# Top-k attention with a PReLU MLP: fewer semaphore waits of VectorE on itself, ScalarE's exits moved, filler matmuls, output parts paced

## The chip, the cores and the metric

One core of a Trainium2 chip. The metric is device time in microseconds, lower is better: the median of three timed executions. A profiled execution of the same kernel gives the trace. Engines: PE is TensorE (matmuls), PEld its weight load, DVE VectorE, ACT ScalarE, POOL GpSimd, SP the engine that issues most DMAs. A core's engines run side by side, each through its own program in order, and wait for one another at semaphores.

## The reference

```
scores = (q @ k^T) / sqrt(64)                  # batch 8, heads 8, seq 576, head_dim 64
kth    = 32nd largest score of each row
attn   = softmax of the scores >= kth, others dropped
x      = attn @ v, heads side by side          # 4608 tokens x 512
h      = x @ w_in                              # 512 x 2048
g      = max(h, 0) + alpha * min(h, 0)
out    = g @ w_out                             # 2048 x 512
```

## The kernel before

The score rows are cut into 144 "duos": two tiles of 128 rows by 576 columns. For each batch there are 16 duos of two heads with the same 128 rows, and 2 that collect the last 64 rows of four heads (their scores take 12 matmuls instead of 6, their products with v 20 instead of 10). The main loop runs over slots n, and one slot holds a step of several duos at once, so that the engines overlap:

- PE, in this order: `st_av(n-5)` (xo, weights times v), `h_pe` (ph: 8 matmuls of x @ w_in for a part of the MLP), the last 64 columns of the scores of duo n+1 (in `st_exit_1`), `o_pe` (pz: 5 matmuls, a quarter of an output tile), transposes of the next q and k (tps), `st_qk(n+2)` (ps_sc: the other score columns), `lin` (plin: in slots 16 to 23 half of one of four 128-row pieces of w_in * alpha @ w_out), and a second `o_pe` if over 10 parts are queued.
- ACT: the two Signs of duo n-1 (sg; they count the scores above a threshold), `st_exit_1(n+1)` (copies the second score tile out of PSUM to s_sb), two Relus of duo n-2 (r), `st_exit_0(n+1)` (the first score tile), the Exp of duo n-3 (w), copies of tps, and `o_act`, the copy of a finished output tile (o_sb<-pz).
- POOL: y = s * sg of duo n-1, and the two subtractions that follow the Relus.
- DVE, `dve_slot(n)`: the top 32 of each row. Twelve MAX8 over 96 columns each go by turns to `up` (SBUF) and to `lo` in `small`; two min/max steps merge them (bot and th); MAX8 of bot fills th; `eq` prepares the choice for duo n-1; `neg` is -th; MAX8 of neg gives the threshold p; two MAX8 over 576 columns of y refine duo n-1. In between lie the softmax normalisation (rz, x) and gT<-ph, the Relu of the MLP.

`small` is one PSUM tile of 160 columns that holds lo, th, n8, eq and io9. Each instruction that writes it waits for the one before that touched it. The scores have one PSUM buffer (`ps_s`, three banks), ph and tps share two (`ps_h`, tag "h"), and plin and pz share one (`ps_z`). Parts of the output queue in `oq`, each with the number of gT pieces that it needs. All engine calls go through a helper, so every instruction has line 31, and it keeps each engine in the order in which the code is written.

Of the kernel before, what the change touches and what calls it, by code (L numbers as in the profile page):

```python
# [16 lines left out]
BIG = float(2.0 ** 60)  # L17
NG = 6
# [17 lines left out]
def fast_path(tc, q, k, v, moe_w_in, moe_w_out, moe_alpha, out, flag):  # L36
    nc = tc.nc
    B, H, S, D = q.shape
# [22 lines left out]
    on = lambda m: 0 <= m < ND  # L61

    with ExitStack() as ctx:
# [6 lines left out]
        two = pool("two", 2)  # L70
# [6 lines left out]
        ps_h = pool("ps_h", 2, space=PSUM)  # L77
# [27 lines left out]

        small = ps_d.tile([128, 160], FP32, name="small")
        io9 = small[:, 146:155]
        for i in range(9):
            DVE.memset(io9[:, i:i + 1], float(2 * i - 63 + S))
        KT = const.tile([128, 2 * ND], FP32, name="KT")  # L110
        v1s = [const.tile([128, 5, 2, 65], BF16, name=f"v1_{i}") for i in range(2 * KPB)]
        ws = [const.tile([128, 2, 640], BF16, name=f"w_{i}") for i in range(3)]
# [4 lines left out]
        w_lin_b = [const.tile([128, DMODEL], BF16, name=f"w_lin_b{i}") for i in range(4)]  # L117
# [39 lines left out]
        T = {}  # L157
# [29 lines left out]
        def st_exit_0(n):  # L187
            ACT.copy(T["s", n][:, 0, :], T.pop(("ps", n))[:, 0:S])
# [6 lines left out]
        def dve_slot(n, f_late):  # L195

            lo = small[:, 0:48].rearrange("p (i g c) -> p i g c", i=2, g=NG // 2)
            th = small[:, 48:112].rearrange("p (i c) -> p i c", i=2)  # L200
            n8 = small[:, 112:128].rearrange("p (i c) -> p i c", i=2)
            eq = small[:, 128:146].rearrange("p (i c) -> p i c", i=2)
            if on(n):
                s = T["s", n]
                up = two.tile([128, 2, NG // 2, 8], FP32, name="up", tag="up")
                for i in range(2):
                    for g in range(NG):
                        DVE.max(out=(lo if g % 2 else up)[:, i, g // 2, :],
                                in_=s[:, i, GW * g:GW * g + GW])
                        if i == 0 and g == 1:  # L210
                            kt_sum(n - 2)
                if on(n - 5):
                    norm_a(n - 5)


                bot = two.tile([128, 2, NG // 2, 8], FP32, name="bot", tag="bot")
                DVE.tensor_tensor(bot, up, lo[:, :, :, ::-1], ALU.min)
                DVE.tensor_tensor(th[:, :, 0:24].rearrange("p i (g c) -> p i g c", g=NG // 2), up,
                                  lo[:, :, :, ::-1], ALU.max)
                if on(n - 5):  # L220
                    norm_b(n - 5)
                for i in range(2):
                    DVE.max(out=th[:, i, 24:32], in_=bot[:, i, :, :])
            else:
                kt_sum(n - 2)
                if on(n - 5):
                    norm_a(n - 5)
                    norm_b(n - 5)
            if on(n - 1):
                y, p9, cs = T.pop(("y", n - 1)), T.pop(("p9", n - 1)), T.pop(("cs", n - 1))  # L230
                DVE.tensor_tensor(eq, io9.unsqueeze(1).to_broadcast([128, 2, 9]),
                                  cs.unsqueeze(2).to_broadcast([128, 2, 9]), ALU.is_equal)
            if on(n):
                neg = two.tile([128, 2, 32], FP32, name="neg", tag="neg")
                DVE.tensor_scalar(neg, th, -1.0, None, ALU.mult)
            if on(n - 1):
                DVE.max(out=p9[:, 0, 1:9], in_=y[:, 0, :])
            h_dve()
            if on(n):
                for i in range(2):  # L240
                    DVE.max(out=n8[:, i, :], in_=neg[:, i, 0:31])
            if on(n - 1):
                DVE.max(out=p9[:, 1, 1:9], in_=y[:, 1, :])
            if on(n):
                p9n = three.tile([128, 2, 9], FP32, name="p9", tag="p9", bufs=4)
                DVE.tensor_scalar(p9n[:, :, 0:1], n8[:, :, 7:8], -1.0, None, ALU.mult)
                T["p9", n] = p9n
            if f_late:
                h_pe()
                h_dve()  # L250
            if on(n - 1):
                pk = two.tile([128, 2, 9], FP32, name="pk", tag="pk")
                DVE.scalar_tensor_tensor(out=pk, in0=eq, scalar=BIG, in1=p9, op0=ALU.mult, op1=ALU.mult)
                T["pk", n - 1] = pk

        def st_count(n):
# [12 lines left out]
                POOL.tensor_tensor(y[:, i, :], T["s", n][:, i, :], sg[:, i, :], ALU.mult)  # L269
            T["y", n] = y  # L270

        def st_relu(n):
            s = T["s", n]
            r = two.tile([128, 2, S], BF16, name="r", tag="sg", bufs=3)
            for i in range(2):
                ACT.activation(r[:, i, :], s[:, i, :], AF.Relu, bias=KT[:, 2 * n + i:2 * n + i + 1], scale=-BIG)
            T["r", n] = r

        def st_sub(n):
            s, r = T["s", n], T.pop(("r", n))  # L280
            for i in range(2):
                POOL.tensor_tensor(s[:, i, :], s[:, i, :], r[:, i, :], ALU.subtract)

        def st_exp(n):
            w = ws[n % 3]
# [82 lines left out]
        soon, hq, oq, act, stores, now = [], [], [], [], [], [0]  # L368
# [38 lines left out]
        def h_pe():  # L407
            while soon and soon[0][0] <= now[0]:
                hq.append(soon.pop(0)[1])
            if hq and wi_free and not act:  # L410
                hq.pop(0)()

        def h_dve():
            if act:
# [2 lines left out]
                ch["done"] += e_n  # L417

        def o_pe():
            if lin_done and oq and oq[0][0]["done"] >= oq[0][1]:  # L420
                oq.pop(0)[2]()

        def o_act():

# [42 lines left out]
        hold, lin_done, wi_free = {}, [], []  # L467
# [17 lines left out]
        def lin(kk, a):  # L485
            if a == 0:
                hold["z"] = ps_z.tile([128, DMODEL], FP32, name="plin", tag="z")
            z = hold["z"]
            for f in range(8 * a, 8 * a + 8):
                PE.matmul(z, hold["wi", kk // 2][:, f, 128 * (kk % 2):128 * (kk % 2) + 128],  # L490
                          hold["wl", f // 8][:, f % 8, :], start=(f == 0), stop=(f == NFT - 1))
            if a == 1:
                ACT.copy(w_lin_b[kk], z)
                if kk == 1:
                    wi_free.append(1)
                if kk == 3:
                    lin_done.append(1)


        for i in range(4):  # L500
# [4 lines left out]
        for kk in range(4):  # L505
            at((13, 14, 17, 18)[kk], "ld", lambda kk=kk: in_trans(kk))
            for a in range(2):
                at(16 + 2 * kk + a, "lin", lambda kk=kk, a=a: lin(kk, a))

        def run(n, kind, most=99):  # L510
            l = todo.get((n, kind), [])
            for f in l[:most]:
                f()
            if l[most:]:
                todo.setdefault((n + 1, kind), [])[0:0] = l[most:]
# [32 lines left out]
        for n in range(ND + 6):  # L548
            end = n >= ND
            now[0] = n  # L550
            run(n, "ld")
            o_sp()

            if on(n - 5):
                st_av(n - 5)
            h_pe()
            late = len(hq) > (12 if n < 104 else 5) or end

            if on(n - 1):
                st_count(n - 1)  # L560
                st_y(n - 1)
            if on(n + 1):
                st_exit_1(n + 1)
            o_pe()
            run(n, "w")

            dve_slot(n, late)
            if on(n - 2):
                st_relu(n - 2)
                st_sub(n - 2)  # L570
            run(n, "cast")
            if on(n + 1):
                st_exit_0(n + 1)
            if n < 2:
                prep_all(2 + n, ACT.copy, ACT.copy, ACT.copy)
            run(n, "prep", 1)
            if on(n + 2):
                st_qk(n + 2)
            run(n, "lin")
            if len(oq) > 10 or end:  # L580
                o_pe()
            if on(n - 3):
                st_exp(n - 3)
# [304 lines left out]
```

## Time and profile before

| | |
|---|---|
| median of 3 runs (lowest, highest) | 975.07 us (974.66 to 975.44) |
| the profiled execution's own time | 979.5 us |
| its span in the trace | 977.7 us |
| busy: DVE, ACT, PE, POOL | 841.0, 798.5, 790.2, 748.7 us |
| mean granted clock of TensorE | 0.932 of full speed |

Busy time of an engine is the union of its instructions' times. DVE instructions overlap at their ends, so the distance from start to start is what one costs, not its duration.

### The profile page before, as it was taken

What the parts mean: (1) busy time and instruction counts of PE and PEld (TensorE: products, weight loads), DVE (VectorE), ACT (ScalarE), POOL (GpSimd) and SP (SyncE); (2) the same over time, 40 slices, a digit from 0 to 9 for tenths busy, and PEclk for the clock granted to TensorE, in tenths of its full rate; (3) what the DMA queues carried; (4) which work ended last, traced back from release to release, by engine and by line L of the source; (5) the groups of instructions that cost most, each with busy time, mean ns of one, the idle gap of its engine ahead of it and who ended that gap; (6) DMA issues with size and microseconds to landing.
All of it is one profiled execution on the core that took longest, in us unless ns stands there. A gap on an engine that the chain in (4) does not pass through costs nothing.

```text
span 977.7 us, 18322 instructions
## 1 busy us (share of the span) xinstructions
PE 790.2 (81%) x5141; PEld 474.4 (49%) x5214; DVE 841.0 (86%) x4063; ACT 798.5 (82%) x1448; POOL 748.7 (77%) x662
## 2 busy tenths in 40 slices
PE   7657768887898878887889787978889688988786
PEld 5334434454464535554455454645455454555453
DVE  3869986689898989899999998999999999899951
ACT  3779985789798978899889897989798998788840
POOL 1788875588787878698888797889788898787840
PEclk9999688899897999798999997999999999799999
DMA  7687763345564454454555464544455443334351
GB/s 160 166 170 155 136 127 72 76 87 107 85 117 91 93 109 96 87 128 85 120 96 116 83 119 91 102 97 106 100 117 106 91 84 71 66 73 65 79 94 42
DMA packets 341006, 99.35 MB, mean 102 GB/s; under 512 B 333712, under 2 KB 333728, under 8 KB 340896
## 3 DMA queue, kind: packets, MB, share of 16 engines
q1 hardware_dynamic: 337888, 95.40, 48.1%
q0 software_dynamic: 608, 2.11, 1.3%
q10 hardware_dynamic: 2400, 0.59, 0.3%
q8 instruction: 43, 0.70, 0.3%
q14 instruction: 67, 0.55, 0.2%
HBM read 36.71 MB, written 9.44 MB: 47 GB/s over the span
## 4 chain that ended last, share of the span: by engine, by line
DVE 57%; PE 20%; ACT 12%; issue 4%; DMA 3%; POOL 1%; another core or an unknown queue 1%; SPq 1%; DVEq 0%; ACTq 0%; POOLq 0%
DVE small L31 18%; DVE p L31 15%; DVE up L31 8%; PE ps_sc L31 7%; PE pz L31 6%; DVE gT L31 6%; ACT sg L31 4%; ACT s_sb L31 3%; ACT r L31 3%; PE xo L31 3%; DVE neg L31 2%; DMA wT<-w 2%; DVE x L31 2%; PE ph L31 2%; PE plin L31 2%
## 5 line engine op out<-in xcount | busy, mean ns | idle before, releaser
L31 POOL TENSOR_TENSOR y<-s_sb,sg 128x576 f32<-128x576 f32 x288 | 362.0, 1278 | 190.6 <-ACT sg L31 188.7
L31 PE MATMUL ps_sc<-qkT 64*128 64x128 f32 (+7 forms) x1280 | 296.7, 511 | 145.6 <-ACT s_sb L31 142.2
L31 POOL TENSOR_TENSOR s_sb<-s_sb,r 128x576 f32<-128x576 f32 x288 | 362.5, 1280 | 2.3 <-ACT r L31 2.2
L31 PEld LDWEIGHTS ps_sc<-qkT 64*128 64x128 f32 (+1 forms) x1280 | 161.1, 200 | 298.7 <-ACT s_sb L31 200.7
L31 ACT ACTIVATE sg<-s_sb,p 128x576 bf16<-128x576 f32 x288 | 221.0, 770 | 50.8 <-DVE p L31 50.6
L31 DVE MAX8 p<-y 128x8 f32<-128x576 f32 x288 | 215.4, 748 | 2.7 <-POOL y L31 2.3
L31 DVE MAX8 small<-s_sb 128x8 f32<-128x96 f32 x864 | 216.1, 250 | 0.0
L31 DVE MAX8 up<-s_sb 128x8 f32<-128x96 f32 x864 | 211.7, 245 | 1.9 <-ACT s_sb L31 1.9
L31 ACT ACTIVATE r<-s_sb,KT 128x576 bf16<-128x576 f32 x288 | 207.9, 772 | 2.9 <-DVE KT L31 2.9
L31 ACT COPY s_sb<-ps_sc 128x576 f32<-128x576 f32 x288 | 180.0, 625 | 33.2 <-PE ps_sc L31 32.9
L31 ACT ACTIVATE w<-s_sb 128x1152 bf16<-128x1152 f32 x144 | 168.3, 1169 | 1.0 <-POOL s_sb L31 1.0
L31 PE MATMUL pz<-w_out_b,gT 128*128 128x512 bf16 x567 | 156.6, 400 | 12.8 <-issue 10.5
L31 PE MATMUL ph<-xT,w_in_b 128*128 128x256 bf16 (+1 forms) x1216 | 155.8, 274 | 0.1
L31 PE MATMUL xo<-v,wT 128*128 128x65 bf16 (+3 forms) x1600 | 132.1, 203 | 12.5 <-DMA wT<-w 12.5
L31 PEld LDWEIGHTS <-wT 128*128 128x128 bf16 (+3 forms) x1600 | 95.6, 102 | 67.6 <-DMA wT<-w 14.1
L31 PEld LDWEIGHTS <-w_in_b 128*128 128x128 bf16 x1216 | 105.7, 99 | 20.1
L31 DVE TENSOR_SCALAR gT<-ph 128x512 bf16<-128x512 f32 x144 | 97.2, 675 | 17.0 <-PE ph L31 16.9
L31 PEld LDWEIGHTS <-gT 128*128 128x128 bf16 x576 | 58.6, 102 | 65.2 <-issue 14.2
L31 DVE RECIPROCAL rz<-xo 128x2 f32<-128x2 f32 x144 | 22.7, 158 | 52.6 <-PE xo L31 52.6
L31 ACT COPY o_sb<-pz 128x512 f32<-128x512 f32 x36 | 21.1, 586 | 55.5 <-PE pz L31 47.5
L31 DVE MAX8 small<-neg 128x8 f32<-128x31 f32 x288 | 56.5, 196 | 5.0
L31 DVE MAX8 small<-bot 128x8 f32<-128x24 f32 x288 | 54.5, 189 | 5.2
(47 smaller groups left out, 578.5 us busy)
## 6 DMA issues: line engine op xcount, KB each, us to landing
k_st<-in_k_dram SPq DMA_DIRECT2D x64, 128.0 KB, 2.8
v_st<-in_v_dram SPq DMA_DIRECT2D x64, 128.0 KB, 2.6
out_dram<-o_sb SPq DMA_DIRECT2D x32, 256.0 KB, 2.3
q_st<-in_q_dram SPq DMA_DIRECT2D x60, 128.0 KB, 2.7
w_st<-in_moe_w_out_dram SPq DMA_DIRECT2D x4, 1024.0 KB, 6.4
wT<-w SPq DMA_TRANSPOSE x144, 3.5
w_in_b<-in_moe_w_in_dram POOLq DMA_DIRECT2D x4, 512.0 KB, 6.5
k_st<-in_k_dram SPq DMA_DIRECT2D x32, 32.0 KB, 2.6
```

The costliest lines, as they stand in the source:

```text
L31: return self.tc.keep_in_program_order(f(*a, **kw))
```

## The change

Six edits, all in the attention path:

1. The dependencies on `small` are declared by columns (`sm`): an instruction keeps only the waits for those that share columns (or bot, neg, p9) with it.
2. `st_relu` and `st_sub` become one function per tile, and `st_exit_0` is written between the two Relus.
3. `keep_warm`: four bf16 matmuls of 512 columns into a PSUM tile of tag "h" that nobody reads, after `h_pe` where that had nothing to do, and after `st_qk` where `o_pe` had nothing to do and there is no `lin`.
4. The second `o_pe` of a slot runs only if over 9 parts are ready, and not for the last quarter of a tile.
5. The copy w_lin_b<-plin moves one slot later, behind the second Relu.
6. `o_pe` and `h_pe` return whether they did something.

```diff
+        def sm(ins, reads, writes):
+            meet = lambda x, y: x == y if str in (type(x), type(y)) else x[0] < y[1] and y[0] < x[1]
+            hit = lambda a, b: any(meet(x, y) for x in a for y in b)
+            keep = [r[0] for r in recent
+                    if hit(writes, r[1]) or hit(writes, r[2]) or hit(reads, r[2])]
+            tc.declare_no_dep(ins.ins, group="small", keep=keep, reason="other columns")
+            tc.add_to_no_dep_group("small", ins.ins)
+            recent.append((ins.ins, reads, writes))
...
-                    DVE.max(out=th[:, i, 24:32], in_=bot[:, i, :, :])
+                    o = 48 + 32 * i
+                    sm(DVE.max(out=th[:, i, 24:32], in_=bot[:, i, :, :]), [f"bot{n % 2}"], [(o + 24, o + 32)])
...
+        def ready():
+            k = 0
+            while lin_done and k < len(oq) and oq[k][0]["done"] >= oq[k][1]:
+                k += 1
+            return k
+
+        def keep_warm():
+            ps = ps_h.tile([128, 512], FP32, name="idle", tag="h")
+            for i in range(4):
+                PE.matmul(ps, v1s[0][:, 0, :, :].rearrange("p a b -> p (a b)")[:, 0:128], ws[0][:, 0, 0:512],
+                          start=(i == 0), stop=(i == 3))
...
+        def lin_out(kk):
+            ACT.copy(w_lin_b[kk], hold["z"])
...
+            at(18 + 2 * kk, "lin_out", lambda kk=kk: lin_out(kk))
...
-            h_pe()
+            if not h_pe() and not end and n > 3:
+                keep_warm()
...
-            o_pe()
+            did = o_pe()
...
             if on(n - 2):
-                st_relu(n - 2)
-                st_sub(n - 2)
-            run(n, "cast")
+                st_relu(n - 2, 0)
             if on(n + 1):
                 st_exit_0(n + 1)
+            if on(n - 2):
+                st_relu(n - 2, 1)
+            run(n, "cast")
+            run(n, "lin_out")
...
-            run(n, "lin")
-            if len(oq) > 10 or end:
+            if (n, "lin") in todo:
+                run(n, "lin")
+            elif not did and not end and n > 3:
+                keep_warm()
+            elif end or (ready() > 9 and oq[0][1] < NFT):
                 o_pe()
```

On VectorE, in a slot of the middle of the program, these stood from the normalisation x to the threshold's MAX8 (in brackets the semaphores waited for; DVE_49 is VectorE's own):

```order
L31 TENSOR_TENSOR x<-xo,rz 128x128 [waits DVE_49]
L31 MAX small<-bot 128x8 [waits DVE_49] x2
L31 TENSOR_TENSOR small<-small,cs 128x18 [waits DVE_49,Activation_49]
L31 TENSOR_SCALAR neg<-small 128x64 [waits DVE_49]
L31 MAX p_7194<-y 128x8 [waits Pool_49]
L31 TENSOR_SCALAR gT<-ph 128x512 [waits PE_49]
L31 MAX small<-neg 128x8 [waits DVE_49] x2
```

and now stand:

```order
L31 TENSOR_TENSOR x<-xo,rz 128x128 [waits DVE_49]
L31 MAX small<-bot 128x8 [waits DVE_49]
L31 MAX small<-bot 128x8
L31 TENSOR_TENSOR small<-small,cs 128x18 [waits Activation_49]
L31 TENSOR_SCALAR neg<-small 128x64 [waits DVE_49]
L31 MAX p_6755<-y 128x8 [waits Pool_49]
L31 TENSOR_SCALAR gT<-ph 128x512 [waits PE_49]
L31 MAX small<-neg 128x8 [waits DVE_49]
L31 MAX small<-neg 128x8
```

The order is the same; the second MAX8 of bot, `eq` (small<-small,cs) and the second MAX8 of neg lost their wait on VectorE, and so did the MAX8 from s_sb into `small`, six in a slot, above these. `neg` still waits, now for the MAX8 of bot.

On ScalarE these stood in slot 17, where the first piece of w_lin was copied:

```order
L31 COPY s_sb<-ps_sc 128x576 [waits PE_49,Activation_49]
L31 ACTIVATE r<-s_sb,KT 128x576 [waits DVE_49,Pool_49]
L31 ACTIVATE r<-s_sb,KT 128x576
L31 COPY s_sb<-ps_sc 128x576 [waits PE_49]
L31 CAST w_lin_b_154<-plin 128x512 [waits PE_49]
```

and now in slot 18:

```order
L31 COPY s_sb<-ps_sc 128x576 [waits PE_49,Activation_49]
L31 ACTIVATE r<-s_sb,KT 128x576 [waits DVE_49,Pool_49]
L31 COPY s_sb<-ps_sc 128x576 [waits PE_49]
L31 ACTIVATE r<-s_sb,KT 128x576
L31 CAST w_lin_b_154<-plin 128x512
```

The second exit stands ahead of the second Relu in every slot, and the cast comes a slot after its matmuls, behind the Relus.

On PE behind the scores of duo 36 (slot 34), a part of the output stood ahead of the products with v:

```order
L31 MATMUL ps_sc<-qkT 128x128
L31 LDWEIGHTS xT
L31 MATMUL pz<-w_lin_b_157,xT 128x512
L31 LDWEIGHTS gT [waits DVE_49]
L31 MATMUL pz<-w_out_b_151,gT 128x512
```

and now the products with v follow at once:

```order
L31 MATMUL ps_sc<-qkT 128x128
L31 LDWEIGHTS wT [waits DMAHW7_49]
L31 MATMUL xo<-v_4_137,wT 128x65 [waits DVE_49]
```

So it is throughout: behind the scores stood a part in 41 slots, now in one. In each of the slots 25 to 141 there is now one part behind the last score columns, where before 37 of these 117 had none. Behind the last slot's scores 130 matmuls of pz are left, before 105. There are 34 groups of filler matmuls: 28 in slots 4 to 19, two each in most of these, and 6 later.

## Rows read from the trace of the kernel before

**Rows 1.** The page: the chain that ended last, shares by engine.
```profile
DVE 57%; PE 20%; ACT 12%; issue 4%; DMA 3%; POOL 1%; another core or an unknown queue 1%; SPq 1%; DVEq 0%; ACTq 0%; POOLq 0%
```

**Rows 2.** Windows: stretch, us, busy of PE, PEld, DVE, ACT, POOL; PEclk, DMA, GB/s.
```profile
0.00:130.36 130.36, 88.05 (x379) 54.08 (x379) 98.90 (x472) 100.81 (x185) 88.20 (x99) 0.93 0.77 155
130.36:202.69 72.33, 58.42 (x348) 33.76 (x351) 50.78 (x251) 50.29 (x93) 46.39 (x40) 0.85 0.43 85
202.69:780.26 577.57, 482.87 (x3270) 290.75 (x3317) 533.86 (x2610) 506.52 (x924) 480.39 (x414) 0.94 0.50 101
780.26:933.74 153.48, 128.88 (x873) 75.44 (x887) 143.61 (x703) 130.44 (x234) 126.19 (x104) 0.93 0.39 75
933.74:977.70 43.96, 31.95 (x279) 20.35 (x282) 13.83 (x32) 10.41 (x16) 7.50 (x6) 0.96 0.27 63
```

**Rows 3.** Groups on DVE, 202.69 to 933.74: xcount, busy us, mean ns, idle before.
```profile
L31 DVE TENSOR_TENSOR small<-small,cs 128x18 f32<-128x18 f32 x118 | 21.7, 184 | 15.2 <-ACT sg L31 3.4 <-DVE small L31 0.5
L31 DVE RECIPROCAL rz<-xo 128x2 f32<-128x2 f32 x118 | 18.5, 157 | 24.4 <-PE xo L31 24.4
```

**Rows 4.** Groups on ACT, the same stretch.
```profile
L31 ACT ACTIVATE sg<-s_sb,p 128x576 bf16<-128x576 f32 x237 | 181.9, 770 | 48.8 <-DVE p L31 48.7
...
L31 ACT COPY o_sb<-pz 128x512 f32<-128x512 f32 x31 | 18.2, 586 | 30.1 <-PE pz L31 30.0
```

**Rows 5.** Timeline of DVE, one slot: start us, us, instruction.
```profile
495.25 0.25 DVE L31 MAX8 up<-s_sb 128x8 f32<-128x96 f32 x1
...
495.82 0.25 DVE L31 MAX8 small<-s_sb 128x8 f32<-128x96 f32 x1
495.98 0.24 DVE L31 MAX8 up<-s_sb 128x8 f32<-128x96 f32 x1
496.14 0.25 DVE L31 MAX8 small<-s_sb 128x8 f32<-128x96 f32 x1
...
497.82 0.41 DVE L31 MAX8 small<-bot 128x8 f32<-128x24 f32 x2
498.33 0.18 DVE L31 TENSOR_TENSOR small<-small,cs 128x18 f32<-128x18 f32 x1
498.56 0.23 DVE L31 TENSOR_SCALAR neg<-small 128x64 f32<-128x64 f32 x1
...
499.95 0.43 DVE L31 MAX8 small<-neg 128x8 f32<-128x31 f32 x2
500.29 0.74 DVE L31 MAX8 p<-y 128x8 f32<-128x576 f32 x1
...
501.16 0.25 DVE L31 MAX8 up<-s_sb 128x8 f32<-128x96 f32 x1
```

**Rows 6.** The chain of waits, same slot: the second MAX8 of each pair.
```profile
498.04 0.20 DVE small L31
...
500.18 0.20 DVE small L31
```

**Rows 7.** Timeline of ACT at a long slot that began at 358.29.
```profile
361.33 0.59 ACT L31 COPY o_sb<-pz 128x512 f32<-128x512 f32 x1 [3.90 <-PE pz L31]
```

**Rows 8.** Timeline of PE there.
```profile
356.42 3.63 PE L31 MATMUL ps_sc<-qkT 64*64 64x512 f32 x12 [1.43 <-ACT s_sb L31]
...
360.26 1.03 PE L31 MATMUL pz<-w_out_b,gT 128*128 128x512 bf16 x4
...
365.88 2.05 PE L31 MATMUL ps_sc<-qkT 64*64 64x512 f32 x12 [0.35 <-ACT s_sb L31]
...
372.08 1.24 PE L31 MATMUL ps_sc<-qkT 64*128 64x512 f32 x6
```

**Rows 9.** Window of one ordinary slot with ph, pz and tps.
```profile
489.36:495.25 5.89, 4.80 (x35) 3.02 (x34) 5.68 (x29) 5.54 (x11) 4.99 (x4) 1.00 0.30 58
```

**Rows 10.** Groups on ACT, 130.36 to 202.69.
```profile
L31 ACT CAST w_lin_b<-plin 128x512 bf16<-128x512 f32 x4 | 2.3, 586 | 12.7 <-PE plin L31 12.7
```

**Rows 11.** Timeline of PE in start-up.
```profile
56.41 1.06 PE L31 MATMUL xo<-v,wT 128*128 128x65 bf16 x10 [5.28 <-DMA wT<-w]
```

More of the change, by code (lines that the diff above doesn't have):

```diff
@@ L107, in fast_path @@
         io9 = small[:, 146:155]
+        recent = []
+        def sm(ins, reads, writes):
[6 more added lines that the diff above has]
+            recent.append((ins.ins, reads, writes))
+            del recent[:-60]
         for i in range(9):
-            DVE.memset(io9[:, i:i + 1], float(2 * i - 63 + S))
+            sm(DVE.memset(io9[:, i:i + 1], float(2 * i - 63 + S)), [], [(146 + i, 147 + i)])
         KT = const.tile([128, 2 * ND], FP32, name="KT")
@@ L207, in dve_slot @@
                     for g in range(NG):
-                        DVE.max(out=(lo if g % 2 else up)[:, i, g // 2, :],
-                                in_=s[:, i, GW * g:GW * g + GW])
+                        o = 24 * i + 8 * (g // 2)
+                        m = DVE.max(out=(lo if g % 2 else up)[:, i, g // 2, :],
+                                    in_=s[:, i, GW * g:GW * g + GW])
+                        if g % 2:
+                            sm(m, [], [(o, o + 8)])
                         if i == 0 and g == 1:
@@ L216, in dve_slot @@
                 bot = two.tile([128, 2, NG // 2, 8], FP32, name="bot", tag="bot")
-                DVE.tensor_tensor(bot, up, lo[:, :, :, ::-1], ALU.min)
-                DVE.tensor_tensor(th[:, :, 0:24].rearrange("p i (g c) -> p i g c", g=NG // 2), up,
-                                  lo[:, :, :, ::-1], ALU.max)
+                sm(DVE.tensor_tensor(bot, up, lo[:, :, :, ::-1], ALU.min), [(0, 48)], [f"bot{n % 2}"])
+                sm(DVE.tensor_tensor(th[:, :, 0:24].rearrange("p i (g c) -> p i g c", g=NG // 2), up,
+                                     lo[:, :, :, ::-1], ALU.max), [(0, 48)], [(48, 72), (80, 104)])
                 if on(n - 5):
@@ L230, in dve_slot @@
                 y, p9, cs = T.pop(("y", n - 1)), T.pop(("p9", n - 1)), T.pop(("cs", n - 1))
-                DVE.tensor_tensor(eq, io9.unsqueeze(1).to_broadcast([128, 2, 9]),
-                                  cs.unsqueeze(2).to_broadcast([128, 2, 9]), ALU.is_equal)
+                sm(DVE.tensor_tensor(eq, io9.unsqueeze(1).to_broadcast([128, 2, 9]),
+                                     cs.unsqueeze(2).to_broadcast([128, 2, 9]), ALU.is_equal),
+                   [(146, 155)], [(128, 146)])
             if on(n):
                 neg = two.tile([128, 2, 32], FP32, name="neg", tag="neg")
-                DVE.tensor_scalar(neg, th, -1.0, None, ALU.mult)
+                sm(DVE.tensor_scalar(neg, th, -1.0, None, ALU.mult), [(48, 112)], [f"neg{n % 2}"])
             if on(n - 1):
@@ L240, in dve_slot @@
                 for i in range(2):
-                    DVE.max(out=n8[:, i, :], in_=neg[:, i, 0:31])
+                    o = 112 + 8 * i
+                    sm(DVE.max(out=n8[:, i, :], in_=neg[:, i, 0:31]), [f"neg{n % 2}"], [(o, o + 8)])
             if on(n - 1):
@@ L245, in dve_slot @@
                 p9n = three.tile([128, 2, 9], FP32, name="p9", tag="p9", bufs=4)
-                DVE.tensor_scalar(p9n[:, :, 0:1], n8[:, :, 7:8], -1.0, None, ALU.mult)
+                sm(DVE.tensor_scalar(p9n[:, :, 0:1], n8[:, :, 7:8], -1.0, None, ALU.mult), [(112, 128)], [f"p9{n % 4}"])
                 T["p9", n] = p9n
@@ L252, in dve_slot @@
                 pk = two.tile([128, 2, 9], FP32, name="pk", tag="pk")
-                DVE.scalar_tensor_tensor(out=pk, in0=eq, scalar=BIG, in1=p9, op0=ALU.mult, op1=ALU.mult)
+                sm(DVE.scalar_tensor_tensor(out=pk, in0=eq, scalar=BIG, in1=p9, op0=ALU.mult, op1=ALU.mult),
+                   [(128, 146), f"p9{(n - 1) % 4}"], [])
                 T["pk", n - 1] = pk
@@ L270, in st_y, with st_relu @@
             T["y", n] = y
-        def st_relu(n):
+        def st_relu(n, i):
             s = T["s", n]
[L274 to L282, printed above, removed]
+            if i == 0:
+                T["r", n] = two.tile([128, 2, S], BF16, name="r", tag="sg", bufs=3)
+            r = T["r", n]
+            ACT.activation(r[:, i, :], s[:, i, :], AF.Relu, bias=KT[:, 2 * n + i:2 * n + i + 1], scale=-BIG)
+            POOL.tensor_tensor(s[:, i, :], s[:, i, :], r[:, i, :], ALU.subtract)
         def st_exp(n):
@@ L411, in h_pe @@
                 hq.pop(0)()
+                return True
+        def ready():
[8 more added lines that the diff above has]
+                          start=(i == 0), stop=(i == 3))
         def h_dve():
@@ L419, in o_pe @@
         def o_pe():
-            if lin_done and oq and oq[0][0]["done"] >= oq[0][1]:
+            if ready():
                 oq.pop(0)[2]()
+                return True
         def o_act():
@@ L491, in lin @@
                           hold["wl", f // 8][:, f % 8, :], start=(f == 0), stop=(f == NFT - 1))
[L492 to L497, printed above, removed]
+            if a == 1 and kk == 1:
+                wi_free.append(1)
+        def lin_out(kk):
+            ACT.copy(w_lin_b[kk], hold["z"])
+            if kk == 3:
+                lin_done.append(1)
         for i in range(4):
```

## The prediction

> **What bounds the kernel now.** I read the chain of waits first: it lies on DVE for 57% of the span, on PE for 20% and on ACT for 12% [rows 1]. The windows then split the span into four parts [rows 2]: start-up (slots 0 to 16, 130.4 us), the w_lin slots 17 to 25 (72.3 us), the steady slots 26 to 143 (577.57 + 153.48 = 731.05 us for 118 slots, 6.195 us each), and a tail of 44 us that PE fills.
>
> In the steady part an ordinary slot lasts 501.16 - 495.25 = 5.91 us and DVE never stops in it [rows 5]. 118 x 5.905 = 697 us, so 34 us come on top. Their names are in the groups: DVE waited 24.4 us for xo of PE [rows 3], and ACT 30.0 us for a finished pz [rows 4]. The second is the first seen from the other end. At 358.29 a long slot begins: PE ran 12 score matmuls in 3.63 us where the same 12 took 2.05 one slot later, so it was at half clock; a part of the output stood behind them, ACT stood 3.90 us at o_sb<-pz, and the slot lasted over 8 us [rows 7, 8]. ACT itself waits for DVE 48.7 us [rows 4], so it is next in line: it works 506.52 us in the first 93 steady slots, 5.45 each, and 130.44 in the last 25, 5.22 each [rows 2].
>
> **VectorE's waits.** From start to start [rows 5, 6]:
>
> - An MAX8 of 96 columns without a wait on DVE (up at 495.98) starts 0.16 us after the one before; one with a wait (small at 496.14) also 0.16. The six waits among the twelve are already met, so removing them gives 0.
> - The two MAX8 of bot start 0.22 apart (497.82, 498.04), `eq` 0.29 behind (498.33), `neg` 0.23 behind that (498.56). Without waits I use the hand-over from the second MAX8 of neg to p, which has no wait on DVE that is still open: 500.29 - 500.18 = 0.11, a little less for 24 columns than for 31: 0.10. Then the second MAX8 starts at 497.92 and `eq` at 498.02. `neg` still needs the second MAX8, which takes 0.20, and a wait that is met ends 0.03 after its cause (498.04 against 497.82 + 0.19): 498.15 in place of 498.56, 0.41 less.
> - The two MAX8 of neg start 0.23 apart, then 0.11: 0.12 less.
>
> Sum 0.52 us a slot: DVE's slot falls from 5.905 to 5.39. Lower bound 0, by the 96-column rows; I take 0.52, because these pairs follow each other directly, as the 96-column waits do not. On VectorE the Trainium skill speaks against this (VectorE: DVE Perf Modes, "The DRAIN you can't avoid"): it measured that a chain of copies takes the same time with a semaphore after each, and advises to cut the number of operations and not semaphores. By it this term is 0. The trace agrees for the 96-column rows (0.16 and 0.16) and differs for the short ones (0.22 against 0.11).
>
> **Steady slots.** With DVE at 5.39, ACT is the longer in the first 93 slots (5.446 by its work) and DVE in the last 25: 93 x 5.446 + 25 x 5.39 = 641 us is the floor. What comes on top is PE's. An ordinary slot holds 4.80 us of PE work at full clock [rows 9], which fits in 5.45 with some 0.2 us of hand-overs at the exits. About 26 slots (four in each batch of 18) hold twelve score matmuls (2.05 us where six take 1.24 [rows 8]) or twenty for xo: about 5.8 us, 0.4 over: 10 us. Some 8 slots with a second ph are 0.5 over: 4 us. I leave 8 us, my choice, for stretches at half clock, which these windows now have (mean 0.94 and 0.93 [rows 2]). Steady: 641 + 22 = 663 us, 5.62 a slot, 68 less than before. That the excess of 34 us goes is the pacing of the parts: one per slot, and no last quarter behind the scores, so ACT no longer finds pz unfinished. Bounds: 641 (nothing over) and 693 (5.87 a slot, the second rival).
>
> The exit between the Relus adds no ACT work. It brings the scores' buffer free one Relu earlier, which covers PE's long slots. Its cost is that PE's last score columns have one Relu to hide behind, not two; that is the second rival.
>
> **w_lin slots.** ACT's four waits for plin, 12.7 us [rows 10], go when the copy is a slot later; the matmuls are long done then, and the next piece can't start before it, which costs PE half a microsecond behind the scores, under cover of them. I take 13 us: 72.3 to 59. ACT's work there is 50.3 us [rows 2], so 22 is the most; the least is 5, if PE, at granted clock 0.85, stays the limit.
>
> **Start-up.** Of the filler, 28 of 34 groups lie in slots 4 to 19. Four matmuls of this shape took 1.03 us at full clock with the end of the last [rows 8], so a group keeps PE for about 0.9, double at half clock. In most slots I expect PE to wait that long anyway for ACT's exits, since it is busy only 88 of the 130 us [rows 2]. Where xo comes late from a transposing DMA (5.28 us at 51 to 56 us [rows 11]) the second group lies behind it and ahead of columns that ACT waits for: 1 to 1.7 us in about four slots, 5 us. VectorE's 0.5 in some nine slots is 4.5 back. I take 0, between -5 and +6.
>
> **Tail.** 25 more pz matmuls are left for it, at most 1.03 / 4 = 0.26 us each [rows 8]; as their ends overlap I take 0.22: +5.4 us.
>
> **Sum.** 979.5 + 0 - 13 - 68 + 5.4 = 904 us for the profiled execution. The median of the runs is 975.07, 0.9955 of the profiled 979.5, so 900 us.
>
> **Rivals.**
>
> - *The waits cost nothing* (0.08). The short MAX8 would hold the next instruction as long anyway, as a drain. For it: the 96-column rows. Against it: 0.11 behind the second MAX8 of neg. Then DVE's slot stays 5.905: of the 34 us 24 go, w_lin gives 10, the tail takes 5.4: 979.5 - 34 + 5.4 = 951, median 947.
> - *PE bounds every slot* (0.13). Exit 0 of ACT needs PE's last columns, which start after exit 1. If PE is 0.4 us late there in each slot, ACT loses it each time: 5.45 + 0.4 = 5.85, steady 690, sum 979.5 - 41 - 10 + 5.4 = 934, median 930. For it: PE has 4.8 us of work plus hand-overs. Against it: at 5.91 it still had a microsecond to spare [rows 9].
> - *Half clock* (0.04), slower than before. If shorter slots and waits leave PE at half clock for over a third of the steady part, its 4.8 + 0.2 us become 5.0 / 0.81 = 6.2 and no slot is shorter than the 6.195 of now. At half of the time they become 6.7: 118 x 6.7 = 791, sum 979.5 + 60 + 5.4 = 1045. It decides at a mean granted clock of 0.81. Against it: the steady part now has 0.93 to 0.94 [rows 2], and after the change no slot there is without a part of the output. The Trainium skill (TensorE: Matmul & The Clock Gate, "The HAM clock gate") says that the clock is low unless PE is active; by it filler and even parts raise the clock.
>
> **How the numbers follow.** My forecast has 0.73: 880 to 918, with the bounds 641 and about 675 of the steady part and those of w_lin and start-up partly together. With most of the second rival the range becomes 878 to 934. A measurement here can tell about 0.2% from no change: faster 0.95, the same 0.01, slower 0.04.
>
> **What would show it.** On DVE: the second MAX8 of bot 0.10 behind the first, `neg` about 0.33 behind the first, and ordinary slots of 5.4 to 5.6 us. On ACT: the idle time before sg for DVE falls, that before o_sb and w_lin_b nearly goes, and ACT is busy about 90% of the steady part. PE's granted clock there is 0.95 or more. A slot of 5.9 us with short MAX8 at 0.22 would be the first rival; ACT idle before s_sb for PE, beyond 30 us in the steady part, the second; a granted clock under 0.85 the third.

## The result, and the profile after

The changed kernel takes 901.52 us (median of 4 runs, 901.29 to 904.88), the kernel before 975.26 on the same chip: ratio 0.9247 (this kernel's time over the other's), 95% interval 0.9219 to 0.9275. The forecast was 900. The profiled execution took 901.29 us, with a span of 899.5. Of the runs below, one of e3 and one of e11, each about 1.5% above the fastest of its kernel, count in the median and not in the ratio.

The windows of the changed kernel, cut at the same slots as those of before [rows 2]; start-up is split at the start of slot 5 (us, busy PE, PEld, DVE, ACT, POOL, PEclk, DMA, GB/s):

```profile
0.00:51.65 51.65, 36.10 (x133) 22.71 (x133) 29.99 (x136) 30.01 (x58) 22.84 (x39) 0.68 0.70 154
51.65:145.35 93.70, 68.12 (x349) 33.84 (x348) 66.56 (x337) 69.63 (x126) 65.00 (x59) 0.79 0.66 131
145.35:202.45 57.10, 52.09 (x343) 29.93 (x343) 48.36 (x251) 50.12 (x93) 46.52 (x40) 0.97 0.56 108
202.45:849.88 647.43, 584.63 (x4224) 352.09 (x4221) 635.82 (x3314) 631.65 (x1158) 607.28 (x520) 0.99 0.55 108
849.88:899.50 49.62, 37.70 (x308) 22.73 (x305) 13.11 (x30) 10.43 (x17) 7.50 (x6) 0.96 0.26 61
```

| stretch | before | after | difference | forecast |
|---|---|---|---|---|
| start-up, slots 0 to 16 | 130.36 | 145.35 | +15.0 | 0 |
| w_lin, slots 17 to 25 | 72.33 | 57.10 | -15.2 | -13 |
| steady, slots 26 to 143 | 731.05 | 647.43 | -83.6 | -68 |
| tail | 43.96 | 49.62 | +5.7 | +5.4 |
| span | 977.7 | 899.5 | -78.2 | -75.6 |

Two terms were off by 15 us each, in opposite directions. So the total came out right by luck, and start-up and the steady part need an explanation of their own.

The page's chain of waits after, shares by engine, for comparison with [rows 1]:

```profile
DVE 33%; ACT 25%; PE 22%; POOL 7%; issue 6%; DMA 5%; SPq 1%; ACTq 0%; POOLq 0%
```

DVE no longer holds over half of the chain; ACT now has about as much as PE. The groups of the steady part on ACT (202.45 to 849.88), answering to [rows 4]:

```profile
L31 ACT ACTIVATE sg<-s_sb,p 128x576 bf16<-128x576 f32 x237 | 184.1, 789 | 6.2 <-DVE p L31 5.7
L31 ACT COPY s_sb<-ps_sc 128x576 f32<-128x576 f32 x234 | 150.4, 643 | 8.2 <-PE ps_sc L31 7.5
...
L31 ACT COPY o_sb<-pz 128x512 f32<-128x512 f32 x30 | 17.9, 596 | 0.0
```

and on DVE, answering to [rows 3]:

```profile
L31 DVE TENSOR_TENSOR small<-small,cs 128x18 f32<-128x18 f32 x118 | 19.8, 168 | 1.2 <-ACT sg L31 0.8
L31 DVE RECIPROCAL rz<-xo 128x2 f32<-128x2 f32 x119 | 18.5, 155 | 3.9 <-PE xo L31 3.5
```

ACT's idle time for p of DVE fell from 48.7 to 5.7 us, that for pz from 30.0 to 0, and DVE's for xo from 24.4 to 3.5. The mark of the second rival, over 30 us of ACT waiting for the scores, is 7.5. An ordinary slot on DVE, from up to up, answering to [rows 5] (start us, us, instruction; a pair is one row):

```profile
458.02 0.25 DVE L31 MAX8 up<-s_sb 128x8 f32<-128x96 f32 x1
458.19 0.25 DVE L31 MAX8 small<-s_sb 128x8 f32<-128x96 f32 x1
...
460.59 0.27 DVE L31 MAX8 small<-bot 128x8 f32<-128x24 f32 x2
460.76 0.17 DVE L31 TENSOR_TENSOR small<-small,cs 128x18 f32<-128x18 f32 x1
460.89 0.22 DVE L31 TENSOR_SCALAR neg<-small 128x64 f32<-128x64 f32 x1
...
462.29 0.28 DVE L31 MAX8 small<-neg 128x8 f32<-128x31 f32 x2
462.48 0.74 DVE L31 MAX8 p<-y 128x8 f32<-128x576 f32 x1
...
463.35 0.25 DVE L31 MAX8 up<-s_sb 128x8 f32<-128x96 f32 x1
```

The slot lasts 463.35 - 458.02 = 5.33 us in place of 5.91. From the first MAX8 of bot to `neg` it takes 0.30 us (before 0.74), from the first MAX8 of neg to p 0.19 (before 0.34). The median of the slots 26 to 142 is 5.330 against 5.907.

That median is not what the whole part costs. Here it is divided as in the forecast, into the first 93 slots and the last 25:

```profile
202.45:712.17 509.72, 458.09 (x3311) 278.00 (x3307) 500.47 (x2610) 501.16 (x924) 479.98 (x416) 0.99 0.59 114
712.17:849.88 137.71, 126.54 (x916) 74.09 (x915) 135.35 (x706) 130.49 (x235) 127.30 (x105) 1.00 0.43 84
```

and the longest of ACT's waits in the first of them (us in total, times, longest):

```profile
ACT s_sb L31 <- PE ps_sc L31: 5.1, 8, 1.1
```

In the first 93 slots ACT works 501.16 of 509.72 us, 5.39 a slot, which is more than DVE's median slot. It waits for 7.4: these 5.1 and 1.3 for tps, both for PE, and 1.0 for p of DVE. So ACT's work is the floor there, with DVE's (500.47) hardly lower; in the last 25 slots it is DVE's, 135.35 of 137.71.

### The profile page after: what moved, and what is told of

It is laid out like the page before. It is cut to its first block, busy times and chain, and to the rows that moved or that the text cites. A ratio compares the mean times of both kernels' runs of the same rounds, so it can differ in the third digit from the quotient of the medians.

```text
span 899.5 us, 18557 instructions
## 1 busy us (share of the span) xinstructions
PE 778.6 (87%) x5350; PEld 461.3 (51%) x5350; DVE 793.8 (88%) x4063; ACT 791.8 (88%) x1448; POOL 749.2 (83%) x662
## 3 DMA queue, kind: packets, MB, share of 16 engines
q1 hardware_dynamic: 337888, 95.40, 53.4%
## 4 chain that ended last, share of the span: by engine, by line
DVE 33%; ACT 25%; PE 22%; POOL 7%; issue 6%; DMA 5%; SPq 1%; ACTq 0%; POOLq 0%
DVE small L31 9%; DVE p L31 9%; ACT sg L31 7%; PE ps_sc L31 6%; ACT r L31 6%; DVE up L31 5%; ACT w L31 5%; ACT s_sb L31 5%; PE pz L31 5%; POOL y L31 4%; DVE gT L31 4%; PE xo L31 4%; PE ph L31 3%; DMA wT<-w 3%; PE idle L31 2%
## 5 line engine op out<-in xcount | busy, mean ns | idle before, releaser
L31 PE MATMUL ps_sc<-qkT 64*128 64x128 f32 (+7 forms) x1280 | 265.4, 461 | 85.5 <-ACT s_sb L31 82.1
L31 PEld LDWEIGHTS ps_sc<-qkT 64*128 64x128 f32 (+1 forms) x1280 | 148.3, 182 | 227.6 <-ACT s_sb L31 138.2
L31 ACT ACTIVATE r<-s_sb,KT 128x576 bf16<-128x576 f32 x288 | 228.4, 794 | 3.8 <-DVE KT L31 2.6
L31 ACT COPY s_sb<-ps_sc 128x576 f32<-128x576 f32 x288 | 184.6, 641 | 34.3 <-PE ps_sc L31 33.3
L31 PE MATMUL ph<-xT,w_in_b 128*128 128x256 bf16 (+1 forms) x1216 | 150.7, 268 | 0.8 <-DVE gT L31 0.8
L31 PE MATMUL pz<-w_out_b,gT 128*128 128x512 bf16 x576 | 149.6, 383 | 0.0
L31 PEld LDWEIGHTS <-wT 128*128 128x128 bf16 (+3 forms) x1600 | 91.5, 100 | 67.1 <-DMA wT<-w 21.4
L31 ACT ACTIVATION_READ_ACCUMULATOR sg<-s_sb,p 128x1 f32 x288 | 59.7, 207 | 0.0
L31 PE MATMUL pz<-w_lin_b,xT 128*128 128x512 bf16 x144 | 56.3, 391 | 3.8 <-ACT o_sb L31 3.8
L31 ACT COPY qkT<-tps 128x512 f32<-128x512 f32 (+1 forms) x93 | 44.5, 482 | 6.1 <-PE tps L31 6.0
```

Source lines behind the costliest of these rows:

```text
L31: return self.tc.keep_in_program_order(f(*a, **kw))
```

## What had to be told apart

My theory for the gain was the forecast's: open waits of VectorE on the instruction right before cost time, met ones nothing, and the pacing of the parts takes away what PE puts on top. Rivals: the pacing or the higher granted clock gives it all. For the start-up's loss there were three candidates: the filler, through its own time on PE; the filler, through something that waits for it; and the order of exits and Relus. The stretches of all kernels, from the profiled executions. "Steady" goes here from the start of slot 26 to the start of slot 143, and "end" from there on, so that kernels with another tail can be compared:

| kernel | median us | ratio, interval | start-up | w_lin | steady | end |
|---|---|---|---|---|---|---|
| before | 975.26 | | 130.36 | 72.33 | 725.05 | 49.99 |
| after | 901.52 | 0.9247 (0.9219 to 0.9275) | 145.35 | 57.10 | 641.42 | 55.64 |
| e1_no_early_fill | 888.96 | 0.9081 (0.9035 to 0.9127) | 134.24 | 56.85 | 642.32 | 55.21 |
| e2_two_relus_first | 894.70 | 0.9143 (0.9098 to 0.9188) | 140.44 | 57.61 | 641.53 | 55.59 |
| e3_cols_only | 931.72 | 0.9499 (0.9430 to 0.9569) | 130.41 | 69.70 | 678.57 | 50.84 |
| e4_all_waits | 954.96 | 0.9757 (0.9708 to 0.9806) | 145.82 | 57.70 | 694.85 | 56.16 |
| e5_pace_only | 953.43 | 0.9764 (0.9738 to 0.9790) | 129.33 | 69.98 | 696.23 | 55.81 |
| e6_no_fill_relus_first | 882.13 | 0.9035 (0.9002 to 0.9068) | 130.10 | 57.50 | 638.65 | 55.16 |
| e7_lin_in_slot | 913.94 | 0.9372 (0.9343 to 0.9402) | 143.34 | 69.43 | 642.12 | 55.53 |
| e8_late_parts | 888.72 | 0.9089 (0.9056 to 0.9122) | 129.60 | 56.17 | 651.88 | 51.02 |
| e9_met_waits_back | 881.47 | 0.9038 (0.8976 to 0.9100) | 129.83 | 56.95 | 638.16 | 55.18 |
| e10_fill_behind_scores | 897.70 | 0.9178 (0.9118 to 0.9238) | 139.57 | 59.13 | 641.87 | 55.29 |
| e11_fill_scores_v | 887.61 | 0.9099 (0.9045 to 0.9154) | 129.22 | 54.53 | 643.79 | 55.32 |
| e12_fill_all_v | 895.53 | 0.9176 (0.9145 to 0.9208) | 139.09 | 54.18 | 645.25 | 55.45 |

## The experiments on VectorE's waits

**e4_all_waits** is the changed kernel with all waits on `small` as before:

```diff
-            tc.declare_no_dep(ins.ins, group="small", keep=keep, reason="other columns")
-            tc.add_to_no_dep_group("small", ins.ins)
```

> The changed kernel with every wait of VectorE on itself back, all else kept. Theory waits-cost: an ordinary slot is 5.905 us again, and the steady part 118 x 5.905 plus under 10 us = 697 to 707 us instead of 647: total 951 to 961 us. Theory waits-free: 900 to 903 us, and the gain came from the other edits.

DVE in an ordinary slot of this kernel:

```profile
501.03 0.41 DVE L31 MAX8 small<-bot 128x8 f32<-128x24 f32 x2
501.55 0.18 DVE L31 TENSOR_TENSOR small<-small,cs 128x18 f32<-128x18 f32 x1
501.77 0.23 DVE L31 TENSOR_SCALAR neg<-small 128x64 f32<-128x64 f32 x1
...
503.24 0.43 DVE L31 MAX8 small<-neg 128x8 f32<-128x31 f32 x2
503.58 0.74 DVE L31 MAX8 p<-y 128x8 f32<-128x576 f32 x1
```

The 0.74 and 0.34 of before are back, with the new pacing, the filler and the moved exit all in place. Steady: 694.85 against 641.42, so the waits are worth 53.4 us of the change, 0.46 a slot (less than 0.577, since without them ACT's work is the floor of most slots). The granted clock of this part is 0.98, so the clock does not give the gain either. This shows that the first rival is wrong.

**e3_cols_only** keeps the waits by columns alone; `keep_warm`, the moved exit, `lin_out` and the pacing are as before:

```diff
-            if (n, "lin") in todo:
-                run(n, "lin")
-            elif not did and not end and n > 3:
-                keep_warm()
-            elif end or (ready() > 9 and oq[0][1] < NFT):
+            run(n, "lin")
+            if len(oq) > 10 or end:
```

> The kernel before with the column dependencies alone. Theory waits-cost: an ordinary slot falls from 5.905 to 5.33 us, while the long slots (output parts behind the scores, half clock) stay as long as ScalarE and PE make them: steady part 731 to some 680 us, total 920 to 935 us. Theory waits-free (a drain would hold the next instruction as long): ordinary slots stay at 5.9 us, total 973 to 977 us.

Ordinary slots are at 5.337 us, steady at 678.57: 46.5 less than before. Its group on ACT in the steady slots still holds the wait for pz, 23.9 us where [rows 4] have 30.0:

```profile
L31 ACT COPY o_sb<-pz 128x512 f32<-128x512 f32 x31 | 18.3, 589 | 24.0 <-PE pz L31 23.9
```

**e5_pace_only** is the reverse: the pacing alone, no `sm`, no filler, exit and copy of w_lin as before.

> The kernel before with the pacing of the output parts alone (one part behind the last score columns of each slot, no last quarter behind the scores). Theory pacing: the steady slots lose what the changed kernel with all waits back had lost, 725 to about 695 us up to the start of the last slot; the w_lin slots stay near 72 us, start-up near 130, the tail grows by 5 to 6 us: total 945 to 955 us. Rival (the filler or the moved exit took the long slots away, not the pacing): 970 us or more.

Two rows of ACT in its steady slots:

```profile
L31 ACT ACTIVATE sg<-s_sb,p 128x576 bf16<-128x576 f32 x235 | 180.3, 769 | 61.8 <-DVE p L31 61.7
...
L31 ACT COPY o_sb<-pz 128x512 f32<-128x512 f32 x30 | 17.5, 583 | 0.0
```

The wait for pz is gone, and ACT waits for DVE instead, 61.7 us where it was 48.7. Steady 696.23: 28.8 less than before, 5.1 above 117 slots of 5.907. Together the two parts give 725.05 - 641.42 = 83.6, more than 46.5 + 28.8 = 75.3: with slots of 5.3 us the parts behind the scores delay more slots than with 5.9 (43 of 117 are over 0.3 us above the median in e3, 33 before), so the pacing is worth more there. In e5 the granted clock of the steady part was 0.99, as in the changed kernel, yet the median slot stayed at 5.907; only five of 117 are shorter, four of them at 5.31, and those five do no gT. A higher clock alone is no explanation for the shorter slots.

**e9_met_waits_back** takes the version without filler and with both Relus first (e6, below) and gives five of the six 96-column MAX8 that write `small` (all but the first of a slot) a wait on the MAX8 two before, which is met when they come:

```diff
-                            sm(m, [], [(o, o + 8)])
+                            sm(m, [], [(o, o + 8)], after=[(0, 48)])
```

> The kernel without filler and with both Relus first, in which five of the six MAX8 from s_sb into small wait again for the one before (another MAX8 stands between them). If a wait costs only what is still open of it, ordinary slots stay at 5.33 us and the total at 880 to 885 us. If a wait on VectorE costs by itself (a semaphore to be set and read), five a slot at 0.03 us or more are 118 x 0.15 = 18 us or more: 898 us or later.

Steady 638.16 against 638.65 for e6, medians 881.47 and 882.13: no difference. Two neighbours in an ordinary slot of e9, the second with the wait:

```profile
444.27 0.24 DVE L31 MAX8 up<-s_sb 128x8 f32<-128x96 f32 x1
444.43 0.25 DVE L31 MAX8 small<-s_sb 128x8 f32<-128x96 f32 x1
444.59 0.24 DVE L31 MAX8 up<-s_sb 128x8 f32<-128x96 f32 x1
```

Both start 0.16 after the one before. A wait that is met costs nothing that can be measured; one on the short instruction right ahead costs 0.12 to 0.21 us. The Trainium skill (VectorE: DVE Perf Modes, "The DRAIN you can't avoid") reports that in a chain of eight copies a semaphore after each costs nothing extra: the met waits of e9 agree, the open ones of e4 do not.

## The experiments on w_lin, the exit and the parts

**e7_lin_in_slot** puts the copy of w_lin back into the slot of its matmuls:

```diff
+                ACT.copy(w_lin_b[kk], z)
...
-            at(18 + 2 * kk, "lin_out", lambda kk=kk: lin_out(kk))
```

> The changed kernel with the copy of w_lin back in the slot of its matmuls. As I put it, ScalarE's four waits for plin (12.7 us) are the term: slots 17 to 25 last 67 to 71 us instead of 57.1, total 911 to 916 us. Rival: the clock and the shorter slots of VectorE made the 15 us, and the copy's place is worth under 4 us: 901 to 906 us.

ACT in its w_lin slots (143.34 to 212.77), and below it the changed kernel (145.35 to 202.45), both answering to [rows 10]:

```profile
L31 ACT CAST w_lin_b<-plin 128x512 bf16<-128x512 f32 x4 | 2.3, 586 | 10.0 <-PE plin L31 10.0
```

```profile
L31 ACT CAST w_lin_b<-plin 128x512 bf16<-128x512 f32 x4 | 2.3, 575 | 0.0
```

The stretch goes from 57.10 to 69.43: this copy alone is worth 12.3 of the 15.2 us; the waits for plin are 10.0 of it.

**e2_two_relus_first** is the changed kernel with the exit behind both Relus again:

```diff
                 st_relu(n - 2, 0)
+                st_relu(n - 2, 1)
...
-            if on(n - 2):
-                st_relu(n - 2, 1)
```

> The changed kernel with both Relus ahead of the exit again. Theory A: start-up stays near 145 us. Theory B: start-up ends 8 us or more earlier. Both: in the steady slots PE gets the score buffer 0.68 us later, which costs only slots with much PE work; I expect 5 to 15 us more there, so a total of 906 to 916 us by A and 898 to 908 us by B. If the steady part stays at 647 us, the moved exit is worth nothing there.

Steady 641.53 against 641.42: between the Relus the exit gains nothing there. In the start-up it costs 4.9 us (145.35 against 140.44), between what the two theories said, and with the steady part unchanged the median, 894.70, lies below both forecasts.

**e8_late_parts** is e6 (below) with the second part of a slot allowed in the last slots from two ready parts on, to shorten the tail:

```diff
-            elif end or (ready() > 9 and oq[0][1] < NFT):
+            elif end or (ready() > (9 if n < 120 else 1) and oq[0][1] < NFT):
```

> The kernel without filler and with both Relus first, and in addition a second output part per slot from slot 120 on wherever over one part is ready and it isn't the last quarter. If PE has room there (no transposes from slot 119 on), the tail falls by 5 us and the last slots stay: total 879 to 883 us. If the parts make PE late for ScalarE, the last slots grow by what the tail gives back: the same total as without it, or 2 us more.

The end falls by 4.1 us against e6, but steady rises by 13.2, and the median is 6.6 worse, more than either forecast. Of the 13.2 us 9.7 lie in the slots 120 to 142. The other 3.5 lie in the slots 26 to 119, where the two programs are the same: so much can two executions differ. In slot 130 of e8, 10 us long, PE did this:

```profile
759.88 2.29 PE L31 MATMUL ps_sc<-qkT 64*128 64x512 f32 x6
762.10 0.61 PE L31 MATMUL pz<-w_lin_b,xT 128*128 128x512 bf16 x1
762.50 1.67 PE L31 MATMUL pz<-w_out_b,gT 128*128 128x512 bf16 x4
764.10 1.62 PE L31 MATMUL xo<-v,wT 128*64 128x65 bf16 x20
```

The second part lies ahead of the products with v, at half clock at first (six score matmuls in 2.29 us, not 1.24 [rows 8]), and DVE waits 3.45 us for them:

```profile
765.75 0.17 DVE L31 RECIPROCAL rz<-xo 128x2 f32<-128x2 f32 x1 [3.45 <-PE xo L31]
```

So it is the old long slot again. The 5.7 us that the pacing adds to the tail are not to be had in this way.

## The experiments on the start-up

**e1_no_early_fill** is the changed kernel without filler in slots 4 to 19 (`n > 3` becomes `n > 19` in both places).

> The changed kernel without the 28 groups of filler matmuls in slots 4 to 19; the 6 later groups stay. Theory A (the filler stands on PE ahead of score columns that ScalarE waits for, and makes start-up 15 us longer): slots 0 to 16 end at about 131 to 135 us instead of 145.35, total 888 to 892 us. Theory B (the exit between the Relus makes start-up longer, because the second Relu and with it POOL's subtraction and the Exp come behind a late exit): slots 0 to 16 end at 141 us or later, total 897 to 901 us.

**e6_no_fill_relus_first** takes all filler out and puts the exit behind both Relus:

```diff
-            if not h_pe() and not end and n > 3:
-                keep_warm()
+            h_pe()
...
                 st_relu(n - 2, 0)
+                st_relu(n - 2, 1)
```

> The changed kernel without any filler and with both Relus ahead of the exit. If the two losses of start-up add up (11 us for the filler, 5 us for the exit), slots 0 to 16 end at 130 us and the total is 884 to 888 us. If they are one loss (the exit costs only where the filler makes the score columns late), start-up ends at 134 us as without filler alone and the total is 887 to 891 us. If the six later groups of filler or the moved exit help the steady slots after all, these are over 645 us up to the start of the last.

Start-up 145.35, then 134.24 without early filler, then 130.10 with both Relus first: the whole loss of 15 us is found, 11.1 and 4.1. e1 met the numbers of its theory A; whether for the reason given there is what e10 to e12 ask. The windows of e6, its start-up from slot 5 and its steady part to slot 143:

```profile
51.27:130.10 78.83, 52.34 (x252) 29.95 (x253) 66.59 (x337) 69.83 (x128) 65.39 (x60) 0.52 0.81 156
...
187.60:826.25 638.65, 575.96 (x4104) 349.77 (x4161) 628.53 (x3284) 625.38 (x1150) 601.53 (x515) 0.99 0.55 108
```

With the clock at 0.52 in that stretch, nearly all of it at the lower of the two levels, the start-up is as long as before, and shorter than with filler at 0.79. The Trainium skill (TensorE: Matmul & The Clock Gate, "The HAM clock gate") says that the clock is throttled by default and that activity releases it; the traces agree, with 0.71 to 0.83 in the seven kernels that have filler there and 0.52 to 0.56 in the four without it whose record of the clock covers the stretch, but the higher clock did not make up for what the filler cost. And the steady part has 0.99 without any filler. e6 is the best version (e9 equals it): 0.9035 of before, 882.13 us against the 901.52 of the changed kernel.

The kernel before looks as if it had a high clock in its start-up, 0.93 in [rows 2]. It had not. Its trace has no record of the clock ahead of 100.7 us, and the views count such time as full speed. Here it is from 51 to 100 us, and below it e6, which has records there:

```profile
51.00:100.00 49.00, 30.27 (x141) 18.46 (x141) 39.79 (x197) 41.40 (x75) 39.22 (x37) 1.00 0.82 162
51.00:100.00 49.00, 30.57 (x143) 18.65 (x142) 38.85 (x201) 41.71 (x77) 39.25 (x38) 0.50 0.82 163
```

The same matmuls keep PE busy for nearly the same time, and six score matmuls take 2.29 us in both. So TensorE was at the lower level in both, and the two start-ups are no comparison of clocks; that of the whole kernel before, 0.932, is too high for the same reason.

**e10_fill_behind_scores** is e6 with one filler group back, the one behind the score columns where no part of the output was due. My theory then was that only the other place, ahead of columns that ACT waits for, does harm.

```diff
-            elif not did and not end:
-                pass
+            elif not did and not end and n > 3:
+                keep_warm()
```

> The kernel without filler and with both Relus first, with filler again, but only behind the scores (13 groups, 12 of them in slots 5 to 16, ahead of the products with v); none between these and the last score columns. If filler costs by its place ahead of the columns that ScalarE waits for, this place costs little, because xo waits for a DMA or ScalarE's exits lie ahead: slots 0 to 16 end at 130 to 132 us, total 882 to 885 us. If it costs because PE is busy wherever it stands, half of the 10 to 11 us comes back: start-up 135 us, total 887 to 889 us.

That theory fell, and the other forecast was too low as well: start-up 139.57, 9.5 us more than e6, and 897.70 us in all. Its waits of ACT in the start-up (us in total, times, longest):

```profile
ACT w L31 <- issue: 11.2, 3, 4.3
...
ACT w L31 <- POOL s_sb L31: 2.4, 1, 2.4
```

The Exp w<-s_sb, which never waited in e6, stands idle for 13.6 us, ahead of the Exps of the duos 3, 6, 9 and 12 (in slots 7, 10, 13 and 16): every third. There are three buffers `ws`, Exp takes them in turn, and the filler's moving operand is `ws[0]`. ACT's program in e10, each Exp with its semaphores:

```
L31 ACTIVATE w_141<-s_sb 128x2x576 [waits DMAHW3_49,PE_49,Pool_49]
L31 ACTIVATE w_142<-s_sb 128x2x576 [waits DMAHW4_49,Pool_49]
L31 ACTIVATE w_143<-s_sb 128x2x576 [waits DMAHW4_49,Pool_49]
```

Only the Exp that writes `ws[0]` (w_141) waits for PE, namely for the last filler to have read it. One such place in e10, on PE and on ACT (one record of the four filler matmuls is missing):

```profile
85.43 1.88 PE L31 MATMUL ps_sc<-qkT 64*128 64x512 f32 x6 [1.31 <-ACT s_sb L31]
87.64 1.49 PE L31 MATMUL idle<-w,v 128*128 128x512 bf16 x3 [0.33 <-issue]
```

```profile
84.74 0.64 ACT L31 COPY s_sb<-ps_sc 128x576 f32<-128x576 f32 x1
89.21 1.16 ACT L31 ACTIVATE w<-s_sb 128x1152 bf16<-128x1152 f32 x1 [3.84 <-issue]
```

The filler ends at 87.64 + 1.49 = 89.13, Exp starts at 89.21. ACT had freed the score buffer with its copy and was ready for Exp at once, but stood still until PE had done the next scores and the filler behind them. The view names "issue" as the releaser; only the operands and semaphores of the program show PE. In the changed kernel the same wait is put down to POOL, 6.9 us (its waits of ACT, 51.65 to 145.35):

```profile
ACT s_sb L31 <- PE ps_sc L31: 15.4, 6, 6.3
ACT w L31 <- POOL s_sb L31: 6.9, 3, 2.8
ACT w L31 <- issue: 1.7, 1, 1.7
```

and in one place of e2 (the same view) to the filler itself:

```profile
ACT w L31 <- PE idle L31: 3.2, 1, 3.2
```

**e11_fill_scores_v** and **e12_fill_all_v** test it by one edit, the first on e10, the second on the changed kernel: the filler reads `v1s[0]`, the values v of one pair of heads, which are written before the loop needs them and then only again for every second batch of 18 slots, not "once" as the text on record has it.

```diff
-                PE.matmul(ps, v1s[0][:, 0, :, :].rearrange("p a b -> p (a b)")[:, 0:128], ws[0][:, 0, 0:512],
+                PE.matmul(ps, v1s[0][:, 0, :, :].rearrange("p a b -> p (a b)")[:, 0:128], v1s[0].rearrange("p c h d -> p (c h d)")[:, 0:512],
```

> The version with the filler only behind the scores of a duo (e10), but its matmuls take their moving operand from v1s[0], which is loaded once, and no longer from ws[0], the buffer that Exp of every third duo writes. Theory A (the filler costs time in the start-up because Exp of every third duo must wait until the filler has read its buffer): ScalarE no longer stands still for 2.4 to 4.2 us before w in slots 7, 10, 13 and 16, the start-up falls from 139.6 us to 130 to 132, total 882 to 885 us. Theory B (the filler costs its own time on TensorE, ahead of what the slot needs, whatever it reads): start-up stays at about 139, total about 897 us.

> The changed kernel with that one edit: the filler takes its moving operand from v1s[0] in place of ws[0]. Theory A: start-up from 145.35 us to 135 to 139 (what is left is the order of the exits, 4 to 5 us, and filler ahead of the last score columns), total 891 to 896 us. Theory B: start-up 145, total 901 us.

e11: start-up 129.22, 10.4 less than e10 with the same number of filler matmuls in the same places in the program. ACT's only wait in its start-up is the one for scores:

```profile
ACT s_sb L31 <- PE ps_sc L31: 7.9, 3, 3.6
```

So behind the scores the filler's own time costs the start-up nothing; its operand cost the 10 us. e12: start-up 139.09, 6.3 less than the changed kernel, and the waits of Exp are gone there too. What e12 still has over e1, 139.09 - 134.24 = 4.9 us, is put down to the filler ahead of the last score columns, since that behind the scores cost nothing in e11: ACT waits 19.0 us for scores in e12 against 11.8 in e1. One of the places, in the changed kernel, on PE and on ACT:

```profile
56.87 1.06 PE L31 MATMUL xo<-v,wT 128*128 128x65 bf16 x10 [4.73 <-DMA wT<-w]
57.86 1.89 PE L31 MATMUL idle<-w,v 128*128 128x512 bf16 x4
59.68 0.69 PE L31 MATMUL ps_sc<-qkT 64*128 64x64 f32 x2
```

```profile
60.41 0.64 ACT L31 COPY s_sb<-ps_sc 128x576 f32<-128x576 f32 x1 [6.31 <-PE ps_sc L31]
```

PE waits 4.73 us for the transposed weights (5.28 before [rows 11]), then runs 1.89 us of filler, and only then the columns for which ACT has stood still. The medians of e11 and e12, 887.61 and 895.53, are below those of e10 and the changed kernel (the intervals of e10 and e11 overlap a little, those of the other two do not), and e11, whose start-up is a little below its theory A and whose total is 3 us above it, does not beat e6. Their w_lin slots are 3 us shorter than those of e6, and their steady part is 5 to 7 us longer; why the latter, no run shows, and e6 and e8 differ by 3.5 us in slots where they are the same.

## Why the prediction was right, and where it was not

- **VectorE's waits** (0.52 us a slot): right in kind and a little small. Measured 5.907 - 5.330 = 0.577: bot to `neg` gave 0.44, where I had 0.41 (hand-overs of 0.09, not 0.10), and the pair of neg 0.15, not 0.12. The met waits gave 0, as taken (e9, five of the six).
- **The steady floor** (641): right in form, ACT in the first 93 slots and DVE in the last 25, and 4.5 us too high. Measured the same way it is 501.16 + 135.35 = 636.5: ACT's work is 5.39 a slot and not 5.446, DVE's in the last 25 is 5.41 and not 5.39. The 0.06 us more that VectorE's waits gave bought little, since ACT's work is the floor of most slots.
- **PE on top** (22 us): about half of that, 647.43 - 636.5 = 11. In the first 93 slots ACT waits 6.4 us for PE, where I had 0.4 us for each of about 26 slots; a second ph in a slot costs DVE's own time for a second gT (5.86 us a slot) and stands in its work; and the 8 us for half clock, my choice, are not there (granted 0.99, forecast 0.95 or more).
- **Pacing**: ACT's wait for pz is gone, in e5 also without the rest. Right.
- **w_lin** (-13): -15.2, of which the copy is 12.3 (e7).
- **Tail** (+5.4): +5.7. Right.
- **Start-up** (0, between -5 and +6): the step that failed; +15.0 is outside its own range. Going from before to after by e6, e1 and e12: VectorE's shorter slots -0.3, where I had -4.5 (with these alone, in e3, the start-up is 130.41: it does not follow DVE); the exit between the Relus +4.1, where I had seen a cost only as the second rival, in the steady part; the filler ahead of the columns +4.9, where I had 5; and the filler's operand +6.3, which I had not seen at all. I had read what the filler queues behind it on PE, and not what must wait until it has read its operand. These shares are known to 1 or 2 us: with another order of the edits the exit is 4.9 (e2), and e7, the same program as the changed kernel up to slot 16, starts up in 143.34 and not 145.35.

The total was right by luck: -15.6 against the forecast of the steady part and +15.0 in the start-up cancel. Without the latter the change would have been at e6's 882.

## What to carry to other kernels

An idle engine does not make filler free: its operands are reads, and whoever next writes that buffer waits for them, so feed it from data that is not rewritten meanwhile, and place it behind work that others wait for. Look among same-engine waits for those on the instruction directly ahead and short: these are worth removing (here 0.58 us in 5.9), while met ones are worth nothing. Check a forecast stretch by stretch, since a good total can hide two wrong terms; and read a granted clock beside the time of the matmuls, since a stretch without records is shown as full speed.

## What the runs showed of the hardware

- The hand-over between the short DVE instructions here (MAX8 of 24 and 31 columns, `eq` of 18) is 0.08 to 0.10 us without an open wait, and 0.22 (one semaphore of its own) or 0.29 (its own and ACT's) with one.
- The start-up from slot 5 to 16 takes 78.8 us at a mean granted clock of 0.52 (e6) and 78.2 at 0.78 (e11, with filler behind the scores): the higher clock goes with a start-up only 0.6 us shorter. What sets its length was not tested.
